# Attention inside a fused attention and mixture-of-experts kernel: the three transposes of a step in one group, the tail's in a score bank

## The chip, the cores and the metric

One core of a Trainium2 chip runs the whole program. The metric is the device time of one execution in microseconds, lower is better. The time before is the median of three executions.

## What is computed

The reference runs three layers one after the other. The change touches the first.

```python
# attention: batch 4, heads 8, sequence 576, head size 64, float32
scores = scale * np.matmul(q, k.transpose(0, 1, 3, 2))
...
scores = scores + bias.transpose(2, 0, 1)[None, :, :, :]   # a small network of the positions
scores = scores - np.max(scores, axis=-1, keepdims=True)
attn = np.exp(scores)
attn = attn / (np.sum(attn, axis=-1, keepdims=True) + 1e-09)
return np.matmul(attn, v).astype(np.float32)
...
# layer 2, on 2304 tokens of 512
h = x @ w_in                      # 512 x 2048
g = np.maximum(0.01 * h, h)
return (g @ w_out).astype(np.float32)
...
# layer 3: one of eight experts per token, 512 -> 1024 -> 512, weighted by its gate
```

## The kernel before

The program has three stages. Stage one makes the position bias (matrix multiplies `psb`, line 270, written to DRAM and read back), runs the attention, and fills the gaps between attention steps with the first half of layer 2: `up_units` multiplies finished attention columns by `w_in`, twelve matmuls into a bank `psh` at a time (line 525). It also converts the weights `w_in` and `w_out` from 64-bit words (`w_t`, `wo_t`) on VectorE (DVE). Stage two is the second half of layer 2 (`psx1`, line 784) with the routing. Stage three is the experts. Stages two and three are not touched.

The attention goes in steps. A step is one batch entry, one pair of heads and one block of 128 query rows. For each batch entry come four head pairs with the first 256 rows (half 0: two steps each), then four with the other 320 (half 1: three steps each, the last with 64 rows of both heads side by side, `ib == 4`). That is 80 steps, 64 with two heads' tiles and 16 with `ib == 4`. The pipeline is two steps deep: step n transposes the finished probabilities of step n and computes the scores of step n+2.

The work of a step on TensorE (PE) in the order of the code: `transposes(st, 0)` turns the first head's 512 columns, four 128x128 transposes into a bank `pst`, which one copy moves to `pth` in SBUF; `transpose_tail` turns the last 64 columns of both heads (512 to 640 of the pair) with one transpose into another bank, `psx`, which a small copy moves to `ptt`; `scores(nx, 0)` makes the scores of the first head of step n+2, four matmuls (eight for `ib == 4`) into a two-bank tile `pss`; then comes a filler unit `psh`; then `transposes(st, 1)` for the second head; then `scores(nx, 1)`; then another filler unit. At the end of a group of steps `values` multiplies `pth` and `ptt` by V (`psv`, line 500).

Each `pss` tile is read by a DVE instruction that adds the bias and takes the row maximum (line 418, called the reduction below). ScalarE (ACT) then takes the exponential (line 426), and `normalise` scales the rows: for batch entry 0 on GpSimd (POOL), later on DVE for the first head and ACT for the second. The copies out of `pst` and `psx` are on ACT for entry 0; later DVE copies the first head and the tail, ACT the second head.

PSUM: the pool `psT` has two one-bank buffers, and `pst` and `psx` take turns in them, so three tiles of a step go through two buffers. The pool `psS` has two two-bank buffers for the scores: a tile fills columns 0 to 287 of each of its two 512-column banks.

A tile scheduler sets the final order on each engine from the order of the code and from its own view of when a buffer comes free; each engine then runs its list in that order.

Of the kernel before, what the change touches and what calls it, by code (L numbers as in the profile page):

```python
# [7 lines left out]
F32 = mybir.dt.float32  # L8
# [109 lines left out]
def new_w_in(p):  # L118
    return [p.tile([128, KD, FF // 2], F32R, name=f"wi{k}") for k in range(2)]
# [168 lines left out]
class Attention:  # L288
# [106 lines left out]

    def scores(self, st, h):
        nc, e = self.nc, self.e
        b, hf, p, ib = st  # L400
        kt = self.kv[b, p]
        hi, lo = self.qs[b, hf, p]
        tail = self.qtail[0]
        pr, stat = self.prob[st]
        ps = e.psS.tile([128, 2, 512], F32, tag="s", name="pss")
        o = 128 * (ib - HALVES[hf][2][0])
        if ib == 4:
            ops = [(tail[:, 256 * hh + 128 * k:][:, :128], 640 * hh) for hh in range(2) for k in range(2)]
        else:
            ops = [(t[:, h, o:o + 128], 576 * h) for t in (hi, lo)]  # L410
        for jh in range(2):
            for k, (lhsT, c0) in enumerate(ops):
                nc.tensor.matmul(  # L413
                    ps[:, jh, :288], lhsT=lhsT, rhs=kt[:, c0 + 288 * jh:][:, :288],
                    start=(k == 0), stop=(k == len(ops) - 1),
                )
        prv = pr[:, h].rearrange("p (a j) -> p a j", a=2)
        nc.vector.tensor_tensor_reduce(  # L418
            out=prv, in0=ps[:, :, :288], in1=prv,
            scale=-0.125, scalar=3.0e38, op0=ALU.add, op1=ALU.min, accum_out=stat[:, 0, h:h + 1],  # L420
        )
# [47 lines left out]
        else:  # L469
            COPY[PROB_T[h][b]](nc, ph[:, h, :, o:o + 128], ps.rearrange("p (c i) -> p c i", c=4))  # L470

    def transpose_tail(self, st):

        nc, e = self.nc, self.e
        b, hf, p, ib = st
        pr, _ = self.prob[st]
        pt = self.pt[1]
        o = 128 * (ib - HALVES[hf][2][0])
        ps = e.psT.tile([128, 512], F32, tag="t", name="psx")
        copy = COPY[PROB_T[0][b]]  # L480
        if ib == 4:
            nc.tensor.transpose(ps[0:64, :128], pr[:, 0, 512:576], e.ident)
            for h in range(2):
                copy(nc, pt[64 * h:64 * h + 64, o:o + 64], ps[0:64, 64 * h:64 * h + 64])
            return
        nc.tensor.transpose(ps[:, :128], pr.rearrange("p h j -> p (h j)")[:, 512:640], e.ident)  # L486
        copy(nc, pt[:, o:o + 128], ps[:, :128])
# [75 lines left out]
def phase1(ctx, tc, e):  # L563

    nc = tc.nc
# [3 lines left out]
    at = Attention(nc, e)  # L569
    fl = Filler()  # L570
    groups = [(b, hf, p) for b in range(B) for hf in range(2) for p in range(NP)]
    steps = [g + (ib,) for g in groups for ib in HALVES[g[1]][2]]
# [11 lines left out]
    def side(n, pos):  # L584
        for f, args in todo.pop((n, pos), ()):
            f(*args)
# [51 lines left out]
    loaded = 4  # L638
    for n in range(2):
        for h in range(2):  # L640
            at.scores(steps[n], h)
            at.exps(steps[n], h)
    at.normalise(steps[0])

# [2 lines left out]
    def values_out():  # L647
        nonlocal prev, xs
        if prev is None:
            return  # L650
        pb, ph, pp = prev
        if pp == 0:
            pool = e.xp if ph == 0 else e.late
            xs = [pool.tile([128, KD, HALVES[ph][1]], F32R, tag=f"x{i}{ph}", name=f"x{i}", bufs=1) for i in range(2)]
        at.x_split(prev, *xs)
        if pp == NP - 1:
            fl.add(up_units(nc, e, pb, ph, *xs))
        prev = None

    for n, st in enumerate(steps):  # L660
        g = st[:3]
        b, hf, p = g
        first = start[g] == n
        last = st[3] == HALVES[hf][2][-1]

        quota = 40 * 800.0 / 6.5 if n < 8 else KF * 1600.0 / 8 if hf == 0 else (13 if b == 0 else 17) * 1280.0 / 12
        nx = steps[n + 2] if n + 2 < ns else None
        while loaded < ns and at.free:
            at.load_bias(steps[loaded])
            loaded += 1  # L670
        if first:
            at.new_group()
        at.transposes(st, 0)
        values_out()
        at.transpose_tail(st)
        if nx:
            at.scores(nx, 0)
        if n + 1 < ns:
            at.normalise(steps[n + 1])
        side(n, 0)  # L680
        fl.run(quota / 2)
        if nx:
            at.exps(nx, 0)
        if st[3] != 4:
            at.transposes(st, 1)
        if nx and nx[3] != 4:
            at.scores(nx, 1)
        side(n, 1)
        at.done(st)
        if n == 7:  # L690
            fl.drain()
        else:
            fl.run(quota / 2)
        if nx and nx[3] != 4:
            at.exps(nx, 1)
        if last:
            at.pop_group(g)
            if n == 7:
                early.__exit__(None, None, None)
                e.late = ctx.enter_context(tc.tile_pool(name="late", bufs=1, side="left"))  # L700
                e.wi.append(new_w_in(e.late))
                at.free.append(PROBS)
            at.values(g)
            prev = g
# [681 lines left out]
def program(tc, e):  # L1386
# [4 lines left out]
    with ExitStack() as top:  # L1391
# [16 lines left out]
        for n, b in (("const", 1), ("big", 1), ("small", 4), ("raw", 1), ("kvp", 1), ("ptp", 1)):  # L1408
            setattr(e, n, pool(wide, n, b, side="right"))
        e.psS, e.psT = (pool(wide, n, 2, space=PSUM) for n in ("psS", "psT"))  # L1410
        tail = phase1(up, tc, e)
        wide.close()

# [60 lines left out]
```

## Time and profile before

| what | value |
|---|---|
| median of three runs | 1026.42 us (1024.62 to 1027.13) |
| the profiled execution's own time | 1025.94 us |
| its span in the profile | 1024.1 us |
| PE busy | 980.9 us, 96% |
| DVE busy | 680.3 us, 66% |
| ACT busy | 545.1 us, 53% |
| POOL busy | 101.4 us, 10% |

The profile is of one execution. The busy time of PE contains pipelined matmuls whose ends are modelled, so a matmul's cost is read here from the start of one to the start of the next. A window's row gives, for each engine, the busy time with the number of instructions, then the granted TensorE clock as a share of full speed, the busy share of the DMA engines, and GB/s. The attention runs from about 45 to 520 us of the span: batch entry 0 with half 0 up to about 105, entry 0 with half 1 up to about 165, entry 1 with half 0 up to about 230, and so on.

### The profile page before, as it was taken

What the parts mean: (1) busy time and instruction counts of PE and PEld (TensorE: products, weight loads), DVE (VectorE), ACT (ScalarE), POOL (GpSimd) and SP (SyncE); (2) the same over time, 40 slices, a digit from 0 to 9 for tenths busy, and PEclk for the clock granted to TensorE, in tenths of its full rate; (3) what the DMA queues carried; (4) which work ended last, traced back from release to release, by engine and by line L of the source; (5) the groups of instructions that cost most, each with busy time, mean ns of one, the idle gap of its engine ahead of it and who ended that gap; (6) DMA issues with size and microseconds to landing.
All of it is one profiled execution on the core that took longest, in us unless ns stands there. A gap on an engine that the chain in (4) does not pass through costs nothing.

```text
span 1024.1 us, 19091 instructions
## 1 busy us (share of the span) xinstructions
PE 980.9 (96%) x6294; PEld 807.3 (79%) x6294; DVE 680.3 (66%) x1719; ACT 545.1 (53%) x1102; POOL 101.4 (10%) x112
## 2 busy tenths in 40 slices
PE   5899999999999999999999999999998999999995
PEld 2345778988889988999888888888877888888884
DVE  8888998979865677667766776669983255313312
ACT  5778777546766666555553333344462455424422
POOL 3332421000000000000000000001002111111110
PEclk8999999999999999999999999999999999999998
DMA  7868889989765566545285633437505157312410
GB/s 246 263 201 248 254 282 305 317 269 288 221 205 146 160 188 211 157 141 164 68 259 170 196 113 103 124 117 235 142 21 216 49 198 275 121 42 92 164 41 23
DMA packets 137602, 180.16 MB, mean 176 GB/s; under 512 B 19842, under 2 KB 89858, under 8 KB 137363
## 3 DMA queue, kind: packets, MB, share of 16 engines
q1 hardware_dynamic: 115554, 149.31, 47.4%
q10 hardware_dynamic: 18576, 19.03, 5.3%
q0 software_dynamic: 3360, 10.49, 3.1%
q8 instruction: 52, 0.85, 0.3%
q14 instruction: 60, 0.48, 0.2%
HBM read 196.18 MB, written 43.94 MB: 234 GB/s over the span
## 4 chain that ended last, share of the span: by engine, by line
PE 59%; issue 18%; DMA 12%; DVE 8%; POOL 2%; ACT 1%; SPq 0%; POOLq 0%; DVEq 0%; ACTq 0%
PE psx L784 19%; PE psh L525 15%; PE pss L413 7%; PE psv L500 7%; DMA out_dram<-o,sidx 6%; PE pst L464 5%; PE psb L270 4%; DMA wo_raw<-in_w_out_dram 2%; DVE mk L224 1%; DMA qraw<-in_q_dram 1%; DMA prob<-bias 1%; DVE prob L418 1%; PE psx L486 1%; POOL xg L1241 1%; POOL prob L444 1%
## 5 line engine op out<-in xcount | busy, mean ns | idle before, releaser
L525 PE MATMUL psh<-x,wi 128*128 128x256 f32 (+1 forms) x1536 | 226.8, 298 | 1.7 <-DVE hst L532 1.7
L525 PEld LDWEIGHTS psh<-x,wi 128*128 128x128 f32 x1536 | 211.7, 190 | 3.7 <-DVE hst L532 3.1
L426 ACT ACTIVATE prob<-prob,stat 128x576 f32<-128x576 f32 x144 | 111.3, 773 | 66.4 <-DVE stat L418 55.8
L418 DVE CUSTOM_DVE_ANT_0 prob<-pss,prob 128x576 f32<-128x576 f32 x144 | 107.8, 751 | 22.8 <-PE pss L413 18.7
L784 PE MATMUL psx<-woh,gh 128*128 128x512 f32 x288 | 113.1, 393 | 0.7 <-ACT gh L70 0.7
L784 PE MATMUL psx<-wol,gh 128*128 128x512 f32 x288 | 112.6, 391 | 0.0
L784 PE MATMUL psx<-woh,gl 128*128 128x512 f32 x288 | 112.2, 390 | 0.0
L82 DVE TENSOR_TENSOR htl<-pt,hth 128x512 fp32r<-128x512 f32 x40 | 25.8, 686 | 127.4 <-ACT hth L70 127.4
L70 ACT ACTIVATE gh<-g 128x512 fp32r<-128x512 f32 x72 | 45.4, 632 | 116.4 <-PE psx L784 102.1
L464 PE MATMUL pst<-ident,prob 128*128 128x128 f32 x576 | 89.7, 278 | 4.9 <-DVE pth L78 2.5
L464 PEld LDWEIGHTS pst<-ident,prob 128*128 128x128 f32 x576 | 66.3, 140 | 23.3 <-issue 13.1
L413 PE MATMUL pss<-kt,qhi 128*128 128x288 f32 x256 | 81.7, 334 | 0.0
L1241 POOL DMA_INDIRECT xg<-x,gidx x22 | 23.5, 1067 | 557.6 <-DMA ws<-in_mw_dram 549.0
L270 PE MATMUL psb<-mk,cf 128*32 128x79 f32 (+49 forms) x640 | 61.8, 426 | 12.7 <-POOL cf L254 6.8
L413 PE MATMUL pss<-kt,qlo 128*128 128x288 f32 x256 | 72.6, 298 | 0.0
L500 PE MATMUL psv<-pth,vs 128*64 128x256 f32 (+1 forms) x512 | 71.5, 413 | 0.0
L801 DVE SCALAR_TENSOR_TENSOR junk<-x1s,en 128x512 bf16<-128x512 f32 x96 | 66.0, 687 | 3.5 <-DMA en<-en_d 2.5
L1272 PE MATMUL pu<-w1h,xh 128*128 128x512 f32 x160 | 65.0, 406 | 0.3 <-ACT xh L70 0.3
L70 ACT ACTIVATE pth<-pst 128x512 f32<-128x512 f32 (+1 forms) x100 | 54.5, 549 | 20.1 <-PE pst L464 12.3
L1303 PE MATMUL pd<-w2h,hth 128*128 128x512 f32 x160 | 62.6, 391 | 1.0 <-ACTq L1228 1.0
L784 PEld LDWEIGHTS psx<-woh,gh 128*128 128x128 f32 x288 | 54.1, 188 | 11.8 <-ACT gh L70 1.0
L1272 PE MATMUL pu<-w1l,xh 128*128 128x512 f32 x160 | 63.3, 396 | 0.0
(224 smaller groups left out, 1862.4 us busy)
## 6 DMA issues: line engine op xcount, KB each, us to landing
ws<-in_mw_dram SPq DMA_DIRECT2D x164, 512.0 KB
prob<-bias SPq DMA_DIRECT2D x64, 288.0 KB
g<-h SPq DMA_DIRECT2D x72, 256.0 KB
prob<-bias SPq DMA_DIRECT2D x64, 256.0 KB
bias<-bt SPq DMA_DIRECT2D x36, 295.5 KB
h<-hst ACTq DMA_DIRECT2D x64, 160.0 KB
w_raw<-in_w_in_dram SPq DMA_DIRECT2D x16, 512.0 KB
h<-hst ACTq DMA_DIRECT2D x64, 128.0 KB
```

Of the source, the lines that this page charges most:

```text
L70: nc.scalar.activation(out=out, in_=in_, func=AF.Copy)
L270: nc.tensor.matmul(ps[32 * q:32 * q + 32, :b - a], lhsT=cf[:, 4 * (m % COEF_M) + q], rhs=x, start=True, stop=True, tile_position=(0, 32 * q),)
L413: nc.tensor.matmul(ps[:, jh, :288], lhsT=lhsT, rhs=kt[:, c0 + 288 * jh:][:, :288], start=(k == 0), stop=(k == len(ops) - 1),)
L418: nc.vector.tensor_tensor_reduce(out=prv, in0=ps[:, :, :288], in1=prv, scale=-0.125, scalar=3.0e38, op0=ALU.add, op1=ALU.min, accum_out=st ...
L426: nc.scalar.activation(out=pr[:, h], in_=pr[:, h], func=AF.Exp, bias=stat[:, 0, h:h + 1], scale=-1.0, accum_out=stat[:, 1, h:h + 1],)
L464: nc.tensor.transpose(ps[:, 128 * c:128 * c + 128], pr[:, h, 64 * h + 128 * c:][:, :128], e.ident)
L500: nc.tensor.matmul(ps[64 * h:64 * h + 64, :n], lhsT=vs[:, c, h], rhs=ph[:, h, c, :n] if c < 4 else pt[:, :n], start=(c == 0), stop=(c == 4 ...
L525: nc.tensor.matmul(ps[:, :n], lhsT=w[:, kc], rhs=x[:, kc, :n], start=(k == 0), stop=(k == 3 * KD - 1),)
L784: nc.tensor.matmul(ps, lhsT=a[:, c % 4], rhs=w[:, c], start=(k == 0), stop=(k == 3 * KF - 1))
L801: nc.vector.scalar_tensor_tensor(out=junk, in0=x1, scalar=1.0, in1=e.en[:, k], op0=ALU.mult, op1=ALU.mult, accum_out=e.dots[:, t, k:k + 1],)
L1272: nc.tensor.matmul(ps, lhsT=a[:, k], rhs=w[:, k, c], start=(i == 0), stop=(i == 3 * KD - 1))
L1303: nc.tensor.matmul(ps, lhsT=a[:, k], rhs=w[:, k], start=(k == 0 and j == 0), stop=(k == 7 and j == 2))
```

## The change

The two heads' transposes of a step and the tail's now stand together at the step's start. The tail no longer takes a bank of `psT`: it takes the score tile that will later hold the second head's scores, and is written to columns 288 to 415 of its second bank, which the scores don't use. So a score tile is taken before the tail, the first head's scores take the other one, and the second head's scores come into the tile whose tail was copied out.

```diff
+    def new_scores(self):
+
+        return self.e.psS.tile([128, 2, 512], F32, tag="s", name="pss")
+
+    def scores(self, st, h, ps):
...
-        ps = e.psS.tile([128, 2, 512], F32, tag="s", name="pss")
...
-    def transpose_tail(self, st):
+    def transpose_tail(self, st, ps):
...
-        ps = e.psT.tile([128, 512], F32, tag="t", name="psx")
+        ps = ps[:, 1, 288:416]
...
-            at.scores(steps[n], h)
+            at.scores(steps[n], h, at.new_scores())
...
         at.transposes(st, 0)
         values_out()
-        at.transpose_tail(st)
+        if st[3] != 4:
+            at.transposes(st, 1)
+        ps = at.new_scores()
+        at.transpose_tail(st, ps)
         if nx:
-            at.scores(nx, 0)
+            at.scores(nx, 0, at.new_scores())
...
-        if st[3] != 4:
-            at.transposes(st, 1)
         if nx and nx[3] != 4:
-            at.scores(nx, 1)
+            at.scores(nx, 1, ps)
```

The scheduler's order on PE shows what becomes of it. First, a step of batch entry 1, half 0, as it stands before; each line is an instruction of PE with its line of code, output, inputs and shape, the filler unit left out.

```order
L464 MATMUL pst<-ident,prob 128x128 x4
L486 MATMUL psx<-ident,prob 128x128
L413 MATMUL pss<-kt,qhi 128x288
L413 MATMUL pss<-kt,qlo 128x288
...
L464 MATMUL pst<-ident,prob 128x128 x4
L413 MATMUL pss<-kt,qhi 128x288
L413 MATMUL pss<-kt,qlo 128x288
```

The same step in the changed kernel, on PE:

```order
L467 MATMUL pst<-ident,prob 128x128 x8
L489 MATMUL pss<-ident,prob 128x128
L416 MATMUL pss<-kt,qhi 128x288
L416 MATMUL pss<-kt,qlo 128x288
...
L528 MATMUL psh<-x_853,wi_1482 128x256
L416 MATMUL pss<-kt,qhi 128x288
```

The second head's four transposes moved up over the first head's scores and a filler unit, and the second head's scores now follow directly on the filler unit. The second place is in half 1 of batch entry 1, on PE, in the changed kernel: the step in which the scheduler puts nothing between the two heads' scores.

```order
L467 MATMUL pst<-ident,prob 128x128 x8
L489 MATMUL pss<-ident,prob 128x128
L416 MATMUL pss<-kt,qhi 128x288
L416 MATMUL pss<-kt,qlo 128x288
L416 MATMUL pss<-kt,qhi 128x288
L416 MATMUL pss<-kt,qlo 128x288
L416 MATMUL pss<-kt,qhi 128x288
L416 MATMUL pss<-kt,qlo 128x288
```

The fifth score matmul from the top is the second head's first, and it goes into the tile that the tail's transpose (L489) was written to. The third place is in the first steps of batch entry 1, on PE, in the changed kernel: the last row is the first head's score of the next step.

```order
L416 MATMUL pss<-kt,qhi 128x288
L416 MATMUL pss<-kt,qlo 128x288
L467 MATMUL pst<-ident,prob 128x128 x4
L485 MATMUL pss<-ident,prob 64x128
L528 MATMUL psh<-x_853,wi_1481 128x256
L528 MATMUL psh<-x_854,wi_1481 128x256
L528 MATMUL psh<-x_853,wi_1482 128x256
L416 MATMUL pss<-kt,qhi 128x288
```

Between the second head's scores of one step and the first head's of the next stand only five transposes and three filler matmuls here.

## Rows read from the trace of the kernel before

**Rows 1.** The head of the page: the span.

```profile
span 1024.1 us, 19091 instructions
```

**Rows 2.** Windows of three stretches: busy time (x instructions), TensorE clock, DMA share, GB/s.

```profile
105.00:165.00 60.00, 53.77 (x415) 45.81 (x416) 55.08 (x132) 44.81 (x111) 20.76 (x21) 1.00 0.88 275
165.00:250.00 85.00, 81.41 (x608) 72.70 (x607) 74.10 (x189) 50.70 (x114) 0.00 (x0) 0.98 0.92 297
250.00:500.00 250.00, 249.45 (x1937) 224.13 (x1936) 178.18 (x502) 157.70 (x351) 0.00 (x0) 1.00 0.58 174
```

**Rows 3.** Waits of PE, 100 to 250 us: total us, times, longest.

```profile
PE psx L486 <- issue: 3.3, 2, 2.2
PE pst L464 <- DVE pth L78: 2.5, 1, 2.5
...
PE psx L486 <- ACT pth L70: 1.0, 1, 1.0
PE psx L482 <- ACT pth L70: 0.7, 1, 0.7
PE pst L464 <- ACT pth L70: 0.5, 1, 0.5
```

**Rows 4.** Waits of PE, 250 to 545 us.

```profile
PE psx L486 <- ACT pth L70: 0.5, 2, 0.3
```

**Rows 5.** Timeline, PE and DVE, step at 412 us: start, duration, engine, what.

```profile
410.06 0.30 PE L413 MATMUL pss<-kt,qlo 128*128 128x288 f32 x1
...
410.40 0.76 DVE L418 CUSTOM_DVE_ANT_0 prob<-pss,prob 128x576 f32<-128x576 f32 x1
...
411.95 0.60 PE L464 MATMUL pst<-ident,prob 128*128 128x128 f32 x4
...
412.39 0.27 PE L486 MATMUL psx<-ident,prob 128*128 128x128 f32 x1
...
412.63 0.29 PE L413 MATMUL pss<-kt,qlo 128*128 128x288 f32 x1
...
412.89 0.29 PE L413 MATMUL pss<-kt,qlo 128*128 128x288 f32 x1
...
413.02 1.92 PE L525 MATMUL psh<-x,wi 128*128 128x320 f32 x12
...
413.94 0.28 DVE L78 COPY ptt<-psx 128x128 f32<-128x128 f32 x1
414.14 0.75 DVE L418 CUSTOM_DVE_ANT_0 prob<-pss,prob 128x576 f32<-128x576 f32 x1
...
414.78 0.60 PE L464 MATMUL pst<-ident,prob 128*128 128x128 f32 x4
...
415.36 0.29 PE L413 MATMUL pss<-kt,qlo 128*128 128x288 f32 x1
```

**Rows 6.** Timeline, PE, at 144 us: eight transposes in a row.

```profile
144.16 1.03 PE L464 MATMUL pst<-ident,prob 128*128 128x128 f32 x8
...
145.16 0.29 PE L413 MATMUL pss<-kt,qlo 128*128 128x288 f32 x1
```

**Rows 7.** Timeline, ACT and PE, at 162 and 236 us: tails that waited.

```profile
161.55 0.58 ACT L70 ACTIVATE pth<-pst 128x512 f32<-128x512 f32 x1
...
162.23 0.30 PE L486 MATMUL psx<-ident,prob 128*128 128x128 f32 x1 [2.24 <-issue]
...
236.23 0.33 PE L486 MATMUL psx<-ident,prob 128*128 128x128 f32 x1 [1.02 <-ACT pth L70]
```

**Rows 8.** Timeline, DVE, at 207 us.

```profile
207.31 0.43 DVE L99 TENSOR_SCALAR wo_t<-wo_raw 128x512 uint32<-128x512 uint32 x1 [2.57 <-DMA wo_raw<-in_w_out_dram]
```

**Rows 9.** Windows around 207 us, columns as in rows 2.

```profile
200.00:207.00 7.00, 7.00 (x53) 6.99 (x52) 4.67 (x12) 2.88 (x7) 0.00 (x0) 1.00 0.96 307
210.00:212.00 2.00, 2.00 (x10) 2.00 (x11) 1.30 (x5) 1.31 (x3) 0.00 (x0) 0.50 0.98 312
```

**Rows 10.** Timeline, PE and DVE, at 131 us: a late reduction.

```profile
131.16 0.29 PE L413 MATMUL pss<-kt,qlo 128*128 128x288 f32 x1
...
134.11 0.75 DVE L418 CUSTOM_DVE_ANT_0 prob<-pss,prob 128x576 f32<-128x576 f32 x1
```

More of the change, by code (lines that the diff above doesn't have):

```diff
@@ L394, in load_bias @@
         self.prob[st] = (bt, e.small.tile([128, 2, 2], F32, tag="stat", name="stat"))
-    def scores(self, st, h):
-        nc, e = self.nc, self.e
+    def new_scores(self):
+        return self.e.psS.tile([128, 2, 512], F32, tag="s", name="pss")
+    def scores(self, st, h, ps):
+        nc = self.nc
         b, hf, p, ib = st
```

## Prediction

> **What bounds the kernel now.** I read the windows by stage first, then the waits of PE in the stage that changes, then single steps in the timeline.
>
> The windows show two kinds of attention [rows 2]. From 250 to 500 us PE is busy 249.45 of 250 us at full clock, with DVE at 178 and ACT at 158: PE alone sets the pace there, and whatever takes its time or makes it wait costs at once. From 105 to 250 us PE still has 135.2 of 145 us, but DVE has 129.2, and the DMA engines are at 0.88 and 0.92 of their time. Three resources are nearly full at once, and a wait that is taken from one may come back at another.
>
> The waits of PE say what its missing time is [rows 3]. The change is aimed at the waits for a `psT` buffer. A tail that waits for ACT's copy of `pth` is such a wait, since the tail reads nothing that this copy writes: it waits for the bank. These are 1.0 and 0.7 us; a set of transposes that waits for ACT's copy is another 0.5. Two tails waited 3.3 us in all for something the view can't name. The longer shows it: the copy of `pth` runs from 161.55 for 0.58 us, to 162.13, and the tail starts at 162.23 [rows 7]. I count both as waits for a bank. After 250 us there are two more, 0.5 us together [rows 4]. So the waits for a bank of `psT` are 1.0 + 0.7 + 0.5 + 3.3 + 0.5 = 6.0 us in the whole kernel, 0.6% of its span of 1024.1 us [rows 1].
>
> The 2.5 us behind DVE's copy of `pth` look alike but are another thing [rows 3]. DVE stood 2.57 us before a conversion whose `w_out` data had not landed [rows 8], and its copy was queued behind that.
>
> **What a transpose costs, in a group and alone.** No instruction is added or taken away: the same transposes, the same copies, the same score matmuls and no DMA. The first question is whether PE works faster when nine transposes stand together instead of five and four, since PE then changes once per step, not twice, between transposes and score matmuls. One step answers it [rows 5]. From the first transpose at 411.95 to the second score matmul at 412.63 are 0.68 us for five transposes and one score matmul; a score matmul takes 0.13 (412.63 to 412.89 are two), so a transpose takes 0.11. From 414.78 to 415.36 are 0.58 us for four transposes and one score matmul: 0.45 / 4 = 0.11 again. Eight in a row at 144.16 with one score matmul end at 145.16: (1.00 - 0.13) / 8 = 0.11 [rows 6]. The cost is the same in groups of four, five and eight, so a change of kind costs nothing that is not in this figure. **The regrouping is worth 0 to PE**; its bounds are 0.01 us per step either way, the reading error of these rows, 0.8 us over 80 steps.
>
> **What the lost waits are worth.** The tail no longer needs a bank of `psT`, and the two heads' banks come back once per step. All 6.0 us go as waits for `psT`. But 0.7 + 3.3 + 0.5 = 4.5 us of them lie in batch entry 0 or at its end, where ACT makes all three copies and was late itself. In the changed kernel the second head's scores stand behind ACT's copy of the tail, one filler unit later than the tail stands now. I take half, 2.25 us, as saved by that delay (bounds 0 and 4.5). Of this, what is won before 207 us meets the conversion that waited for its `w_out` data. The DMA engines were 0.96 busy in the 7 us before it [rows 9], so the data come little earlier if PE does; but their 0.88 in the stretch before leaves some room [rows 2]. I keep half again, 1.1 us (bounds 0 and 2.25). The 1.0 us (the tail at 236.23 [rows 7]) and the 0.5 us after 250 lie past that point, the latter where the DMA engines are at 0.58 [rows 2], and I count them in full: 1.5 us. **Gain: 2.6 us**, with 0 and 6.0 as ends.
>
> **What the score banks cost now.** Two things become later or tighter. First, the tail's tile must be copied out before the second head's scores can be written over that bank. Before, the copy of the tail ended at 414.22, 1.83 us after the tail's start at 412.39 [rows 5]. Now the tail starts 0.44 us later (four more transposes) and its copy need not be later, so it ends some 1.4 us after it. The second head's scores come after the tail (0.11), four score matmuls (0.53) and a filler unit (413.02 to 414.78, 1.76 us): 2.4 us. There is 1.0 us of cover in a usual step, and I cost it at nothing. Behind these scores are queued the next filler and all else of PE, so without the cover each microsecond is lost in full.
>
> Second, the tile of the second head's scores is taken until its reduction on DVE ends, and the next step's first scores need it. Before, they needed the one that the first head's scores had left half a step earlier. The way from the last of the second head's scores to the next step's first is now 0.13 + 1.76 + 9 x 0.11 = 2.9 us; with the shorter filler of half 1 (256 columns of 320, so 1.4 us) 2.5 us. The reduction's lag, from the start of the last score matmul to its end, is 1.1 us at 410.06 and 2.0 us at 412.89 [rows 5]. The worst that I find between second-head scores from 105 to 250 us is 131.16 to 134.86, 3.7 us [rows 10]: 1.2 over what it may be. PE waited for POOL just there too, so I take half, 0.6 (bounds 0 and 1.2).
>
> Third, the new order has places with far less cover. I count eight past 250 us, two as in the second piece of order above, and the others like the third, with one to seven filler matmuls in place of a unit. In the third piece, 0.13 + 5 x 0.11 + 3 x 0.12 = 1.04 us stand against a lag of 1.1 to 2.0: a wait of 0.1 to 1.0. In the second, the first matmul that writes into the tail's bank (the scores' third) comes 0.11 + 0.53 + 0.26 = 0.9 us after the tail, against the copy's 1.4. At 412 DVE was late because of other work; where it waits for PE its lag is the shortest, so I go near the lower end, 0.15 us each: 1.2 us (bounds 0 and 8.0). **Loss: 1.8 us**, with 0 and 9.2 as ends.
>
> The load of the next bias tile is issued when all transposes of a step have read their buffer, which is now some 2.3 us sooner (the first scores and a filler). No wait of PE in these views is for a bias tile, so I give it nothing; if it helps, it helps on top.
>
> **Sum.** Against the profiled execution's 1025.94 us: -2.6 + 1.8 = -0.8, 1025.1 us. The profiled execution lies 0.5 us under the median of the three runs (1026.42), so I forecast 1025.6 us, no change that can be measured. What a measurement of this kernel can tell from no change is about 0.3%, 3.1 us.
>
> **The rivals.** *All bank waits stay gone* (faster, 0.31). If ACT catches up in the filler unit, the DMA engines follow and the short places are covered, the whole 6.0 us are won: 1025.94 - 6.0 = 1019.9, by the median 1020.4 us. For it speaks that PE is the fullest engine even from 105 to 250; against it, DVE's 129 of 145 us there.
>
> *The score tiles become the wait* (slower, 0.22 with its neighbours). The place is the turn from the second head's scores to the next step's first, and the tail's copy. It decides from a lag of 1.04 us at the short places and 2.5 to 2.9 at the others. If DVE is late as at 412 at each of the eight, some 0.75 us each, that is 6.0, with 1.2 from the late reduction and only the 1.5 us of sure gain: +5.7, 1031.6, by the median 1032.1 us. For it speaks that DVE is in order and held up by conversions before 250 us; against it the lag of 1.1 us at 410.06, where DVE was free [rows 5].
>
> *The clock falls in the longer groups of transposes* (0.02). PE's clock did fall to its lower level, 1.2 GHz: 0.50 granted from 210 to 212, after the wait of 2.5 us [rows 3, 9]. If nine transposes told like a wait, at least the 656 transposes (64 x 9 + 16 x 5) would take 0.11 us more: 72 us, some 1098. Against it stands the group of eight at 0.11 each, in a stretch with the clock at 1.00 [rows 2, 6]. The Trainium skill, "TensorE: Matmul & The Clock Gate", Part 4 on the transpose by the PE, says that the full clock does not engage for transposes, since they don't count as busy time in the same way. By that rule grouping would be a risk; the trace shows no fall in the groups of eight that it already has.
>
> **How the numbers follow.** No measurable change has 0.45, the first rival 0.31, and slower 0.24 (the second rival 0.22, the clock 0.02). The range goes from the first rival's 1020.4 to 1031.0, just short of the second's price: about 1 in 10 lies beyond each end. The likeliest case alone spans 1023.3 to 1029.5.
>
> **What would show it.** In the profile after, a transpose should still cost 0.11 us start to start in a group of nine; no tail should wait for a copy of `pth`; PE's waits from 105 to 250 us should name the tail's copy `ptt` or the reduction before score matmuls, some 3 us in all; the 2.5 us near 207 should remain, now before scores. After 250 us the score matmuls should wait 1 to 2 us in all. The prediction is wrong if the transposes' cost per piece changes, if score matmuls wait over 5 us in all, or if the scheduler's new order on DVE and ACT moves conversions in front of copies that PE needs, which I have not priced.

## The result and the profile after

The changed kernel takes 1032.34 us (median of 7 runs, 1030.15 to 1037.54), the kernel before beside it 1026.42 us. The ratio is 1.0064 with a 95% interval of 1.0044 to 1.0083: slower by 0.6%, 5.9 us. The profiled execution took 1033.22 us.

The span and the windows of the changed kernel, columns as in [rows 1] and [rows 2]:

```profile
span 1031.4 us, 19091 instructions
...
105.00:165.00 60.00, 57.04 (x430) 46.02 (x429) 52.96 (x129) 45.25 (x112) 17.71 (x19) 1.00 0.86 263
165.00:250.00 85.00, 80.73 (x599) 70.57 (x597) 73.64 (x187) 51.35 (x115) 0.75 (x1) 1.00 0.94 309
250.00:500.00 250.00, 248.43 (x1921) 222.84 (x1920) 176.61 (x498) 160.58 (x348) 0.00 (x0) 1.00 0.57 174
```

From 105 to 165 us PE is busier than before, 57.04 us against 53.77 [rows 2], and still behind. From 250 to 500 it lost a microsecond. The granted clock is 1.00 in all three; before, it was 0.98 from 165 to 250, with the fall to 0.50 near 211 [rows 2, 9].

The waits of PE in the changed kernel, first from 100 to 250 us, then from 250 to 545 (total us, times, longest):

```profile
PE pss L416 <- DVE stat L421: 2.3, 4, 1.1
PE pss L416 <- DVE ptt L78: 2.0, 3, 1.4
PE pst L467 <- issue: 1.4, 1, 1.4
PE pst L467 <- POOL prob L447: 1.0, 2, 0.8
PE pss L416 <- ACT bt L70: 0.2, 1, 0.2
PE pst L467 <- DVE pth L78: 0.2, 1, 0.2
```

```profile
...
PE pss L416 <- DVE stat L421: 1.1, 2, 0.6
PE pss L416 <- DVE ptt L78: 0.5, 1, 0.5
...
```

The waits for a bank of `psT` are gone, all 6.0 us of [rows 3, 4]; the 0.2 us behind DVE's copy of `pth` is of the kind near 207 [rows 8], behind a conversion. The 1.4 us that the view can't name is another thing: DVE's scaling of what these transposes read ended 0.1 us before they started. DVE and PE in the changed kernel:

```profile
242.85 0.51 DVE L445 TENSOR_SCALAR prob<-prob,stat 128x576 f32<-128x576 f32 x1
...
243.47 0.63 PE L467 MATMUL pst<-ident,prob 128*128 128x128 f32 x4 [1.43 <-issue]
```

Score matmuls wait in place of the transposes: 2.3 + 2.0 + 0.2 + 1.1 + 0.5 = 6.1 us, for the reduction (`stat`), for the tail's copy (`ptt`) and, 0.2 us, for a bias copy (`bt`).

A group of nine transposes in the changed kernel's timeline (start, duration, engine, what):

```profile
134.00 1.04 PE L467 MATMUL pst<-ident,prob 128*128 128x128 f32 x8
134.87 0.27 PE L489 MATMUL pss<-ident,prob 128*128 128x128 f32 x1
134.90 0.38 PE L416 MATMUL pss<-kt,qhi 128*128 128x288 f32 x1
135.12 0.29 PE L416 MATMUL pss<-kt,qlo 128*128 128x288 f32 x1
```

From 134.00 to 135.12 are nine transposes and one score matmul: (1.12 - 0.13) / 9 = 0.11 us each, as in groups of four, five and eight [rows 5, 6].

Where the time went is read from the same piece of work in both traces. The fourth `values` group (the end of batch entry 0, half 0) starts 1.5 us later than before, and the first filler unit `psh`, which follows the last bias matmuls, 3.0 us later (114.89 against 111.90). The first `values` of entry 1, half 1 start 3.4 us later (247.26 against 243.83), the last `values` of the attention 4.9 (518.60 against 513.69), the first matmul with `w_out` 5.2 (542.78 against 537.59). So 3.0 us are lost in the first eight steps, 0.4 more up to 248 us, and 1.5 more up to the end of the attention. The last 2.1 us of the profile lie behind the first matmul with `w_out`, in work that the change doesn't touch. In the kernels below that stretch differs from the one before by -0.5 to 2.1 us, and by 2.1 in e5, which from step 8 on is the kernel before, so I take it as what differs from one execution to the next.

### The profile page after: what moved, and what is told of

It reads as the page before. It is cut to its first block, busy times and chain, and to the rows that moved or that the text cites. A ratio compares the mean times of both kernels' runs of the same rounds, so it can differ in the third digit from the quotient of the medians.

```text
span 1031.4 us, 19091 instructions
## 1 busy us (share of the span) xinstructions
PE 989.8 (96%) x6294; PEld 810.0 (79%) x6294; DVE 680.6 (66%) x1719; ACT 548.9 (53%) x1102; POOL 100.7 (10%) x112
## 4 chain that ended last, share of the span: by engine, by line
PE 46%; issue 17%; DMA 17%; DVE 5%; ACT 1%; SPq 1%; POOL 0%; POOLq 0%; ACTq 0%; DVEq 0%
PE psx L789 17%; PE psh L528 13%; DMA out_dram<-o,sidx 7%; PE pss L416 5%; PE psv L503 5%; PE pst L467 4%; DMA wo_raw<-in_w_out_dram 3%; DMA prob<-bias 1%; DVE prob L421 1%; DMA en<-en_d 1%; DMA w_t<-wo 1%; DMA qraw<-in_q_dram 1%; DMA kraw<-in_k_dram 1%; DMA g<-h 1%; PE psdot L818 0%
## 5 line engine op out<-in xcount | busy, mean ns | idle before, releaser
L416 PE MATMUL pss<-kt,qhi 128*128 128x288 f32 x256 | 79.4, 325 | 6.1 <-DVE stat L421 3.3
L467 PE MATMUL pst<-ident,prob 128*128 128x128 f32 x576 | 80.1, 277 | 4.9 <-POOL prob L447 3.1
L467 PEld LDWEIGHTS pst<-ident,prob 128*128 128x128 f32 x576 | 63.7, 140 | 23.0 <-issue 13.5
L503 PE MATMUL psv<-pth,vs 128*64 128x256 f32 (+1 forms) x512 | 75.2, 413 | 0.5 <-ACT bt L70 0.5
L270 PE MATMUL psb<-mk,cf 128*32 128x79 f32 (+48 forms) x640 | 62.5, 429 | 12.4 <-POOL cf L254 6.8
L82 DVE TENSOR_TENSOR gl<-g,gh 128x512 fp32r<-128x512 f32 x72 | 49.3, 688 | 22.7 <-ACT gh L70 18.9
L1308 PE MATMUL pd<-w2l,hth 128*128 128x512 f32 x160 | 63.7, 398 | 0.3 <-DVEq L1233 0.3
```

The lines of the kernel that those rows point to most:

```text
L82: nc.vector.tensor_tensor(out=out, in0=x, in1=hi.bitcast(F32), op=ALU.subtract)
L416: nc.tensor.matmul(ps[:, jh, :288], lhsT=lhsT, rhs=kt[:, c0 + 288 * jh:][:, :288], start=(k == 0), stop=(k == len(ops) - 1),)
L467: nc.tensor.transpose(ps[:, 128 * c:128 * c + 128], pr[:, h, 64 * h + 128 * c:][:, :128], e.ident)
L503: nc.tensor.matmul(ps[64 * h:64 * h + 64, :n], lhsT=vs[:, c, h], rhs=ph[:, h, c, :n] if c < 4 else pt[:, :n], start=(c == 0), stop=(c == 4 ...
L1308: nc.tensor.matmul(ps, lhsT=a[:, k], rhs=w[:, k], start=(k == 0 and j == 0), stop=(k == 7 and j == 2))
```

## The experiments

Two switches set what a step n does. `GROUP(n)`: the second head's transposes are moved up. `BANK(n)`: the tail goes into the score tile. The changed kernel has both in all steps, the kernel before neither. Steps 0 to 7 are batch entry 0, half 0, where the rest of the bias is made between the steps; steps 8 to 19 are its half 1. Each kernel was timed beside the kernel before; the changed kernel's ratio was 1.0064. The last three columns are differences to the trace of before, of one profiled execution each: the start of the fourth `values` group (107.17 us before), of the first one of entry 1, half 1 (243.83) and of the last one (513.69).

| kernel | median us | ratio, 95% interval | 107 | 244 | 514 |
|---|---|---|---|---|---|
| changed | 1032.34 | 1.0064 (1.0044 to 1.0083) | +1.5 | +3.4 | +4.9 |
| e1 grouping alone | 1040.64 | 1.0133 (1.0108 to 1.0158) | +4.7 | +9.4 | +17.1 |
| e2 bank alone | 1028.13 | 1.0011 (0.9995 to 1.0027) | -2.8 | -0.5 | -0.4 |
| e3 both, steps 0 to 7 | 1030.04 | 1.0037 (1.0013 to 1.0061) | +2.3 | +3.8 | +4.0 |
| e4 both, from step 20 | 1030.08 | 1.0025 (1.0008 to 1.0042) | 0.0 | -0.7 | +2.6 |
| e5 bank, steps 0 to 7 | 1025.01 | 0.9981 (0.9958 to 1.0004) | -2.9 | -4.4 | -4.5 |
| e6 whole `values` blocks | 1032.68 | 1.0062 (1.0039 to 1.0085) | +2.0 | +0.8 | +4.2 |
| e7 grouping from step 8 | 1029.27 | 1.0020 (1.0001 to 1.0040) | -2.7 | -2.8 | 0.0 |
| e8 mix | 1027.97 | 1.0002 (0.9983 to 1.0020) | -0.4 | +3.3 | +3.2 |
| e9 no masks, grouped | 1022.91 | 0.9942 (0.9917 to 0.9968) | -10.2 | -4.7 | -2.6 |
| e10 no masks, from 8 | 1022.14 | 0.9935 (0.9914 to 0.9956) | -10.5 | -8.8 | -6.9 |
| e11 copy on DVE, grouped | 1031.59 | 1.0037 (1.0021 to 1.0052) | +2.3 | +3.5 | +5.5 |
| e12 copy on DVE, from 8 | 1032.03 | 1.0041 (1.0022 to 1.0061) | +0.8 | +0.8 | +2.1 |
| e13 late copy, steps 0 to 7 | 1029.88 | 1.0029 (1.0012 to 1.0046) | -1.8 | +2.6 | +4.3 |
| e14 late copy, all steps | 1030.18 | 1.0030 (1.0013 to 1.0047) | -1.9 | +4.6 | +5.6 |
| e15 e13's steps 0 to 7, then before | 1024.59 | 0.9978 (0.9961 to 0.9995) | -1.0 | +0.7 | +0.8 |

The last three columns come from one execution each, and these differ in the granted clock. From 45 to 105 us it is 0.94 in e1, 0.97 in e3, e8, e11 and e15 (in e11 and e15 from 105 to 165 too) and 1.00 in the others; from 165 to 250 it is 0.98 in the kernel before, e1 and e13, 0.96 in e14 and 1.00 in the others. A clock of 0.97 over 60 us is up to 1.8 us (an estimate: 0.03 x 60), so milestones are best compared between kernels of the same clock, and what a kernel takes as a whole is read from the medians. The profiled execution was the slowest run of e1, e8, e9, e11 and e15, and the fastest of e6, e7, e10 and e12.

**Which half of the change loses (e1 to e4).** The first theory was that the shared score tile makes the loss, the rival that the grouping does.

e1:

```diff
 def BANK(n):
-    return True
+    return False
```

> The transposes of both heads and the tail in one group, but the tail back in a bank of psT, and each score tile taken where it was taken before the change. Theory A, the shared score tile makes the loss (scores wait for the tail's copy and for the reduction, and the order is bent around these waits): about the time before, 1025 to 1028 us, with tails that wait for copies of pth again. Theory B, the grouping makes the loss: 1031 to 1033 us.

e2:

```diff
 def GROUP(n):
-    return True
+    return False
```

> The tail in the score tile as in the change, but the second head's transposes where they stood before, after the filler unit. Theory A, the shared score tile: 1030 to 1033 us, with score matmuls that wait for ptt and for the reduction, some 5 us in all. Theory B, the grouping: 1025 to 1028 us.

e3, with the same edit in `BANK`:

```diff
 def GROUP(n):
-    return True
+    return n < 8
```

> The change in the first 8 of 80 steps alone (batch entry 0, half 0, where the bias matmuls fill the gaps), the other 72 steps as before. Theory A by place: in the changed kernel's trace the values of the last group of these steps came 1.5 us later than before and the last bias matmul 4.8 us later, so 1.5 us is the loss here: 1027 to 1029 us. Rival, the early delay is taken back by later waits on transfers: 1025.5 to 1027 us.

e4, with the same edit in `BANK`:

```diff
 def GROUP(n):
-    return True
+    return n >= 20
```

> The change from step 20 on alone (batch entries 1 to 3), entry 0 as before; the scheduler's order on PE is that of before up to step 20. From the changed kernel's trace: entry 1 to 3 lose 0 in the steps at 250 to 460 us and 1.6 us in two waits of scores at 472 and 490 us. Theory A: 1027 to 1029 us. Rival, all the loss is in entry 0, where the other engines are late: 1025 to 1027 us.

The bank alone is no slower (1.0011). The grouping alone costs 13 us, since its three tiles in a row go through the two banks of `psT`. In e1's waits of PE from 100 to 560 us the largest is:

```profile
PE psx L498 <- DVE pth L87: 8.4, 10, 2.7
```

So the bank takes away most of what the grouping adds, and what is left is still the grouping's: the theory fell as the account of the whole, and its rival held, though e1's 1040.64 lies far above the 1031 to 1033 expected of it. The shared tile isn't free, however. In e2's waits of PE from 100 to 555 us the largest is:

```profile
PE pss L425 <- DVE stat L430: 4.4, 5, 1.4
```

Score matmuls wait 5.1 us there with the 0.7 us for `ptt`, about what the bank waits were, and of the 2.8 us that e2 had won at 107 us it keeps 0.5 at 244. By place, e3 and e4 lose 2.7 us each (1030.04 and 1030.08 against 1027.34 for the kernel before beside them), 5.4 of the changed kernel's 5.9; both are about 1 us above the range expected of them.

**The first eight steps, and the cut blocks (e5 to e8).**

e5:

```diff
 def GROUP(n):
-    return True
+    return False
 def BANK(n):
-    return True
+    return n < 8
```

> What it is: the tail's transpose goes into the score tile in the first eight steps only (batch entry 0, half 0); no set of transposes is moved; all later steps are those of the kernel before. Theory C (what is won or lost in the first eight steps is carried to the end, and the bank alone wins there): with the bank in all steps the fourth group's values started 2.8 us earlier than before, and lost this again later; here it should end 2 to 3 us under the kernel before (ratio 0.997 to 0.998). Rival (the 2.5 us wait for the w_out data near 207 us takes back what is won before it): ratio 1.000, the milestones equal from 215 us on.

The profile keeps what was won at 107 us to the end of the attention (-4.5); the median is 2.1 us under the kernel before, and the interval just holds 1.

In the changed kernel the scheduler puts four score matmuls into the `values` blocks of entry 0, half 1. The timeline of the kernel before, and then of the changed kernel, PE:

```profile
138.22 2.37 PE L500 MATMUL psv<-pth,vs 128*64 128x320 f32 x16
140.43 0.71 PE L500 MATMUL psv<-ptt,vs 128*64 128x320 f32 x4
141.06 0.66 PE L464 MATMUL pst<-ident,prob 128*128 128x128 f32 x4
```

```profile
140.54 0.75 PE L503 MATMUL psv<-pth,vs 128*64 128x320 f32 x2
141.22 0.40 PE L416 MATMUL pss<-kt,qhi 128*128 128x288 f32 x1
...
141.95 2.10 PE L503 MATMUL psv<-pth,vs 128*64 128x320 f32 x13
...
144.78 1.09 PE L467 MATMUL pst<-ident,prob 128*128 128x128 f32 x8
```

The whole block takes 141.06 - 138.22 = 2.84 us, the cut one with its four scores 144.78 - 140.54 = 4.24; less 4 x 0.13 that is 3.71, so a cut costs 0.87, and there are three, each of 4.24 to 4.25 us.

e6, in which the steps without the bank are the four with `ib == 4` in entry 0:

```diff
 def BANK(n):
-    return True
+    return not (8 <= n < 20 and n % 3 == 1)
```

> What it is: the changed kernel, except that in the four steps with 64 rows of both heads (ib == 4) of batch entry 0 the tail's transpose takes a bank of psT again, and the second head's scores of the next step but one a tile of their own. The order on PE differs from the changed kernel's by one thing above all: three blocks of 20 matmuls of values in entry 0, half 1 that were cut after the first two by four score matmuls are whole again. Theory D (the cuts cost what the stretch from 110 to 200 us lost though its waits fell): a cut block with its scores took 4.24 us (140.54 to 144.78) against 2.84 for a whole one (138.22 to 141.06 before) and 0.53 for the scores, so 0.87 each, 2.6 us in all: the end 2 to 3 us earlier than the changed kernel, about 1029.5, and the milestone at the start of entry 1 about 2.5 us earlier against it. Rival (the cuts fill time in which PE would wait for the tail's copy anyway): the same as the changed kernel, with waits of scores or of values at those places.

e7:

```diff
 def GROUP(n):
-    return True
+    return n >= 8
```

> What it is: the tail's transpose in the score tile in all steps, as in the changed kernel, but the second head's transposes are moved up only from step 8 on; in the first eight steps they stay behind the first filler unit. Theory C: grouping alone makes the loss in the first eight steps (the changed kernel stood 1.5 us behind at the fourth group's values, the bank alone 2.8 us ahead), so 4 us come off the changed kernel: about 1028, the first w_in matmul about 3 us under that of before. Rival (the loss of the first eight steps is not the grouping's but is made up or lost by chance of order in the next stage): within 1.5 us of the changed kernel.

e8:

```diff
 def GROUP(n):
-    return True
+    return 8 <= n < 20
 def BANK(n):
-    return True
+    return n < 8 or 8 <= n < 20 and n % 3 != 1
```

> What it is: the bank alone in steps 0 to 7, the bank and the grouping in steps 8 to 19 without the cut values blocks (the tail in psT in the four steps with ib == 4), and the kernel before from step 20 on. Theories C and D together: -2.8 us by the fourth group's values, some -1 to -1.5 us in steps 8 to 19 (the waits fell by about 3 us there in the changed kernel, and the cuts are gone), 0 after: 3 to 4 us under the kernel before, about 1023, ratio 0.996 to 0.997. Rival (the conversion of w_out that waits for its data near 207 us takes back all that is won before it): ratio 1.000.

With whole blocks e6's trace gains 3.9 us on the changed kernel from the fourth to the eighth `values` group, more than the 2.6 worked out, but loses most of it again by the second group of entry 1, half 1, and its median is the changed kernel's. The forecast of 1029.5 failed. The first piece that was lost again, 2.1 us up to the ninth group, holds a wait that neither theory named. In e6's timeline, DVE and PE:

```profile
173.29 0.43 DVE L108 TENSOR_SCALAR wo_t<-wo_raw 128x512 uint32<-128x512 uint32 x1 [1.90 <-DMA wo_raw<-in_w_out_dram]
...
175.19 0.68 DVE L87 COPY pth<-pst 128x512 f32<-128x512 f32 x1
...
176.19 0.28 DVE L87 COPY ptt<-pss 128x128 f32<-128x128 f32 x1
...
176.52 0.40 PE L425 MATMUL pss<-kt,qhi 128*128 128x288 f32 x1 [1.75 <-DVE ptt L87]
```

PE came earlier, the `w_out` data did not, DVE stood 1.90 us for them, the tail's copy behind it came late, and the scores waited 1.75 us. e7 takes the grouping out of the first eight steps alone and gains 3.1 us on the changed kernel (1029.27), as expected of the theory that it loses there. e8 is no better than the kernel before, against the 1023 expected: from 107 to 244 us its trace lost 3.7 us, with waits for GpSimd's scaling, the reduction and `psT`. So grouping and bank did not pay in steps 8 to 19 even with whole blocks; e5, without them there, is 3.0 us lower, though the two intervals overlap.

**Why the first eight steps lose (e9 to e12).** From the starts of the matmuls in the trace, from 44.5 us on: the same 326 bias matmuls take 30.0 us before, 31.7 in the changed kernel and 29.9 in e7 (from the start of each to the next matmul's start, summed), and the same 80 `values` matmuls 11.3, 12.5 and 11.7. The transposes take 12.5, 12.0 and 11.9. So the loss against e7 is not in the transposes but mostly in the bias matmuls, which read the masks `mk` that ACT and DVE make. All three traces have the clock at 1.00 there.

e9, in `bias_units`, leaves out 76 of the 144 masks: later blocks read those of block 16 again, which are made 576 columns wide for it. So it computes another bias. e10 has the same and e7's `GROUP`:

```diff
-            if m + 1 < nm:
+            if m >= 16:
+                nxt = mk
+            elif m + 1 < nm:
                 nxt += bias_relu(nc, e, m + 1, (2 * hf, 2 * hf + 1))
```

> What it is: the changed kernel with 76 of the bias network's 144 masks mk left out (the relu instructions of ACT and DVE): the blocks from 17 on multiply the masks of block 16 again, so the bias is another one. The bias matmuls of the first eight steps then never wait for a mask, and ACT and DVE have less to do. It is read against the next kernel, which differs only in where the second head's transposes stand in these eight steps. Theory E (the grouping loses in the first eight steps because masks and bias copies on ACT and DVE come later, so that the four matmuls of a bias group no longer start together: bias matmuls took 1.84 us of the 4 us more there): the two kernels' last bias matmuls and fourth values groups stand within 1.5 us of each other, and the end too. Rival F (it is the order on PE itself, cut values blocks and the wait for GpSimd's scaling of the second head): 3 us or more between them.

> What it is: the same left out as in the run before, with the second head's transposes at their old place in the first eight steps and grouped from step 8 on (the tail in the score tile throughout). Theory E: within 1.5 us of the run before at the last bias matmul, at the fourth values group and at the end. Rival F: 3 us or more earlier than the run before.

e11, in `transposes`; e12 has the same and e7's `GROUP`:

```diff
-            COPY[PROB_T[h][b]](nc, ph[:, h, :, o:o + 128], ps.rearrange("p (c i) -> p c i", c=4))
+            COPY["D" if (b, hf, h) == (0, 0, 1) else PROB_T[h][b]](nc, ph[:, h, :, o:o + 128], ps.rearrange("p (c i) -> p c i", c=4))
```

> What it is: the changed kernel with the copy of the second head's transposes on DVE instead of ACT in the first eight steps, so that three copies no longer stand in a row on ACT. Read against the next kernel, which has the same and the old place of the second head's transposes in these steps. Theory G (the row of three copies on ACT, 0.58 + 0.58 + 0.28 us, is what makes masks and bias copies late): the grouped kernel loses at most 1.5 us against the next one at the last bias matmul and the fourth values group, and is 2 to 3 us faster than the changed kernel. Rival H (the grouping makes all of the step's work on ACT, DVE and GpSimd come in one piece, whichever engine copies): 3 us or more between the two again.

> What it is: the copy of the second head's transposes on DVE in the first eight steps, the second head's transposes at their old place there and grouped from step 8 on, the tail in the score tile throughout. Theory G: within 1.5 us of the run before. Rival H: 3 us or more earlier than it.

Without these masks the bias matmuls cost the same in both orders, 24.0 and 24.2 us, and the medians are 0.8 us apart with overlapping intervals, as theory E has it. The traces agree with it only in part: 0.2 us apart at the fourth `values` group, but 2.2 at the last bias matmul and more later, where e9's is its slowest run and e10's its fastest. With the copy on DVE both orders are equally slow, but because the old order lost its lead (1032.03 against e7's 1029.27), not because the grouped one gained: of theory G, the gain of 2 to 3 us failed. The bias matmuls cost 32.5 us in e11, where the clock was at 0.97, and 34.3 in e12 at 1.00, 4.4 more than in e7 with the same order and the copy on ACT. So the place of this copy matters on DVE too; which of DVE's instructions came late was not looked into.

**The transposes or their copy (e13 to e15).** These keep the transposes grouped in the code and move only the second head's copy back, to where it stood before.

In e13 this holds for n < 8 (`LATE(n)`), in e14 for all steps; e15 is e13 with e3's `GROUP` and `BANK`.

```diff
         if st[3] != 4 and GROUP(n):
-            at.transposes(st, 1)
+            at.transposes(st, 1, not LATE(n))
...
         if nx:
             at.exps(nx, 0)
...
+        if st[3] != 4 and GROUP(n) and LATE(n):
+            at.copy_out()
```

> What it is: the changed kernel, transposes grouped as there, except that in the first eight steps the copy of the second head's transposes stands in the code where it stood before, behind the exponentials, not directly behind the transposes. Theory I (in the first eight steps the grouping loses because the second head's copy is put ahead of the exponentials, the masks and the bias copies on ACT): the fourth values group and the last bias matmul 3 to 4 us earlier than in the changed kernel, the end about 3 us earlier, 1029. Rival J (it loses because the transposes themselves stand together on TensorE, in whatever order ACT works): within 1.5 us of the changed kernel.

> What it is: the same late copy of the second head in all steps. Theory I: 3 to 4 us under the changed kernel, about 1029, as the run before; from entry 1 on the second copy is on ACT and the tail's on DVE, so that there it should change less than 1 us. Rival J: within 1.5 us of the changed kernel.

> What it is: grouping, tail in the score tile and the late copy of the second head in the first eight steps; the kernel before in all later ones. Read against the run that has the changed steps there with the early copy (4.1 us behind the kernel before in its profile). Theory I: the loss in the first eight steps goes, 0 to -2 us against the kernel before, about 1026. Rival J: still 2.5 to 4 us behind it.

One place shows it. At 72.5 us PE starts the same bias matmuls in both kernels, 24 in a row in e13; in the changed kernel the scheduler has put the last four behind score matmuls. The timeline of ACT, DVE and PE in the changed kernel, and then in e13:

```profile
72.32 1.12 DVE L107 SCALAR_TENSOR_TENSOR w_t<-w_raw,w_t 128x512 uint32<-128x512 uint32 x1
72.35 0.59 ACT L70 ACTIVATE pth<-pst 128x512 f32<-128x512 f32 x1
72.53 2.67 PE L270 MATMUL psb<-mk,cf 128*32 128x175 f32 x20
72.83 0.28 ACT L70 ACTIVATE ptt<-pss 128x128 f32<-128x128 f32 x1
73.10 0.32 ACT L70 ACTIVATE bt<-psb 128x175 f32<-128x175 f32 x1
73.31 1.20 ACT L222 ACTIVATE mk<-lw,v 128x432 f32<-128x432 f32 x2
...
74.04 1.20 DVE L224 TENSOR_SCALAR mk<-lw,v 128x432 f32<-128x432 f32 x2
...
75.12 0.40 PE L416 MATMUL pss<-kt,qhi 128*128 128x288 f32 x1
```

```profile
72.02 0.93 DVE L237 TENSOR_SCALAR mk<-lw,v 128x432 f32<-128x432 f32 x1
72.08 0.28 ACT L83 ACTIVATE ptt<-pss 128x128 f32<-128x128 f32 x1
...
72.25 0.65 ACT L235 ACTIVATE mk<-lw,v 128x432 f32<-128x432 f32 x1
...
72.50 1.70 PE L283 MATMUL psb<-mk,cf 128*32 128x175 f32 x24
...
74.13 0.40 PE L429 MATMUL pss<-kt,qhi 128*128 128x288 f32 x1
```

In the changed kernel the second head's `pth` stands ahead of the tail's copy, the bias copy and the mask: ACT's mask of 432 columns starts at 73.31 instead of 72.25, and PE needs 2.59 us for 20 bias matmuls instead of 1.63 for 24. The copy itself is 0.5 us of this (72.35 to 72.83); the rest is that the mask now stands behind the bias copy too. DVE's mask, which the last four matmuls need, starts at 74.04 instead of 72.02, behind a conversion and a reduction. Weight loads name the masks too. Waits of the weight loads, 44.5 to 118 us, in the kernel before, the changed kernel and e13:

```profile
PEld psb L270 <- ACT mk L222: 1.5, 4, 0.4
...
PEld psb L270 <- DVE mk L224: 0.6, 2, 0.4
```

```profile
PEld psb L270 <- ACT mk L222: 2.2, 6, 0.6
...
PEld psb L270 <- DVE mk L224: 1.6, 4, 0.6
```

```profile
PEld psb L283 <- ACT mk L235: 1.4, 3, 0.6
PEld psb L283 <- DVE mk L237: 1.1, 3, 0.6
```

For masks they are 2.1, 3.8 and 2.5 us; the bias matmuls cost 30.0, 31.7 and 29.2. e13 is 3.3 us earlier than the changed kernel at the fourth `values` group, both at clock 1.00, and 2.5 us lower in the median. e15 against e3 is the cleanest pair, since in the code only this copy's place differs: 1024.59 against 1030.04 us, ratios of 0.9978 (0.9961 to 0.9995) and 1.0037 (1.0013 to 1.0061). At the fourth `values` group they too are 3.3 us apart, both at clock 0.97, and their bias matmuls cost 29.0 and 33.3 us. Theory I holds, with 5.5 us between the medians of this pair, or 4.5 when each is taken against the kernel before beside it (1026.35 and 1027.34), where 3 to 4 were expected.

What the pairs show is the place of the copy with all that the scheduler makes of it. The transposes of the first eight steps stand in 17 pieces on PE in the changed kernel and in 18 in e13, against 25 before, so the grouping is still there; but the `values` matmuls stand in 12 pieces in the changed kernel and e3, in 10 in e13 and e15, in 9 before. How much of the gain comes through ACT's queue alone was not separated.

e14 is no faster than e13: from step 8 on the place of that copy changes nothing that can be told apart. e15 beats the kernel before with its whole interval, by 1.8 us, as no other kernel does that computes the same result. That gain isn't the grouping's: e5, with the bank alone in the same eight steps, has a ratio of 0.9981.

## Why the prediction was wrong

Forecast was no measurable change, 1025.6 us; measured were 1032.34, 1.3 us beyond the range's upper end.

**The step that failed** is "the regrouping is worth 0 to PE". Its measurement was right: a transpose costs 0.11 us in a group of nine too. Its conclusion was not, because the step priced what moved on PE and not the copies that go with the transposes. In the order of the code the second head's copy came ahead of the exponential, and on ACT, in the first eight steps, ahead of masks and bias copies for which PE waits. The place of that copy is worth 2.5 of the changed kernel's 5.9 us (e13), and 4.5 to 5.5 where the later steps are those of before (e15 against e3). The text named an order of DVE and ACT that it had not priced as what would make it wrong; it looked for conversions in front of copies, and in these steps it was a copy in front of masks. The rows that it read began at 100 us, behind the place.

**The term that was mis-sized** is the loss of 1.8 us, of which 0 was for the tail's copy, 0.6 for the late reduction and 1.2 for the short places. As waits these are 2.0, 2.3 and 1.6 us, 5.9 in all, and the text's own sign of being wrong, score matmuls that wait over 5 us, came true with 6.1. How much of the lost time these waits make is not shown: e2's score matmuls wait 5.1 us, and e2 is no slower than the kernel before.

**The bank waits** did go, all 6.0 us. What of it would be kept was put at 2.6. From 100 to 250 us all waits of PE fell from 3.3 + 2.5 + 1.2 + 1.0 + 0.7 + 0.5 + 0.5 + 0.3 = 10.0 us (those of [rows 3] and three smaller ones that have no row there: 1.2 and 0.5 for GpSimd, 0.3 for a bias copy) to 7.1, which is 2.9. But 2.3 of that is the one wait near 207 that the forecast said would stay; all the others together fell by 0.6, so from 100 to 250 us most of what the banks gave back came again as other waits. Three cut `values` blocks, 2.6 us, which the step did not see although the order shows them, stand against it too; e6, which has them whole, was no faster, so that they decide the time isn't shown.

**The tail's copy**, costed at nothing for 1.0 us of cover, did cost: 2.0 us in three waits from 100 to 250 us. The longest, in the changed kernel's timeline, DVE and PE:

```profile
218.20 1.92 PE L528 MATMUL psh<-x,wi 128*128 128x320 f32 x12
218.55 0.68 DVE L103 SCALAR_TENSOR_TENSOR wo_t<-wo_raw,wo_t 128x512 uint32<-128x512 uint32 x1
219.26 0.69 DVE L107 SCALAR_TENSOR_TENSOR wo_t<-wo_raw,wo_t 128x512 uint32<-128x512 uint32 x1
...
220.21 0.68 DVE L78 COPY pth<-pst 128x512 f32<-128x512 f32 x1
...
221.13 0.28 DVE L78 COPY ptt<-pss 128x128 f32<-128x128 f32 x1
...
221.47 0.40 PE L416 MATMUL pss<-kt,qhi 128*128 128x288 f32 x1 [1.35 <-DVE ptt L78]
```

The cover was taken from a step at 412 us, and DVE has conversions of `w_out` in front of the copy at 220: here the order that the text named did come.

**The late reduction** was put at 0.6 us and is 2.3, in four waits. **The short places** past 250 us were put at 1.2 and are 1.1 + 0.5 = 1.6, in three waits and not eight: near in size. **The 2.5 us near 207**, said to stay, went: 0.4 us are left there, and 1.35 came at 220. The fall of the clock behind it [rows 9] went too, so the changed kernel is behind although it was spared both in its profiled execution.

**The rivals.** That the score tiles become the wait, 1032.1 us, was right in size and half right in cause: score matmuls do wait 6.1 us, about what the bank waits were, but without the first eight steps the kernel is 2.2 us behind the one before (e7, 1.0020), not 5.7. The clock did not fall in the groups: 1.00 in all three windows. The Trainium skill, "TensorE: Matmul & The Clock Gate", Part 4, on the transpose by the PE, says that the full clock does not engage for transposes. No window here shows that; each holds transposes among other matmuls.

**What stays open.** The larger share of the loss lies from step 8 on, and it is placed but not explained. With the same first eight steps, the later steps of the change cost 5.3 us against those of before (e13 against e15), 4.3 (e7 against e5) and 3.2 (the changed kernel, 5.9 behind, against e3, 2.7 behind). One part is clear in the table. Between its last two columns, at clock 1.00 from 250 to 500 us in every trace, the five kernels that don't group there (e2, e3, e5, e8, e15) stay within -0.1 to 0.2 us of the kernel before, with the bank (e2) or without it; the changed kernel and the nine others with grouping and bank lose 1.0 to 3.4, and e1 7.7. So past 244 us it is the grouping that loses, not the shared tile by itself. e4, which has only the steps from 20 on changed, loses 2.7 us (1.0025). Its waits of score matmuls for the reduction and the tail's copy from 100 to 555 us are 1.8 + 2.6 = 4.4 us, so they are the likely cause, but no run took them away by themselves. What e9 and e10 differ in past the bias was not followed up.

## What to carry to other kernels

When instructions are moved on one engine, price what their results start on the others: list each consumer's old and new neighbours on its own in-order engine, in every stage, the fullest first. Moving the producers and leaving the consumer where it was took that loss away in the first eight steps (e15 against e3); the grouping itself gained nothing that could be measured. A wait taken away where three resources are nearly full can come back at another, as 6.0 us for banks came back as 6.1 for score tiles, so don't count its whole length as gain.

## What was not expected of the hardware

A `values` block that is cut once for four score matmuls costs 0.87 us more than whole (4.24 to 4.25 us each time, three times in the changed kernel), though a change between transposes and score matmuls costs nothing measurable. Bias matmuls are small (each uses 32 of the array's 128 columns) and four of them start within 0.02 us when their masks are there (88.270, 88.277, 88.284 and 88.290 us in the changed kernel, 0.60 us each); when a mask is late, the group falls apart, and 20 took 2.59 us where 24 had taken 1.63. The Trainium skill, "TensorE: Matmul & The Clock Gate", Part 3, says that small matmuls in different tiles of the array can run at the same time. The trace agrees, and shows what is lost when their inputs don't come together.
